# Attention with normalised q and k: per-stretch settings for the written-out order, one norm step fewer, pair scaling in the first group

## The chip, the cores and the metric

The kernel runs on 1 core of a Trainium2 chip. The core has five engines that run their own instruction streams and meet at semaphores: TensorE (PE in the profile; its weight loads are PEld), VectorE (DVE), ScalarE (ACT), GpSimd (POOL) and SyncE (SP), which here issues DMAs. The metric is the device time of one execution in microseconds (us); before the change it is 599.01 us, the median of 3 runs (598.86 to 599.35).

## The reference

32 heads, 2048 positions, 20 features a head, all bf16.

```python
qn = q / (jnp.sqrt((q * q).sum(axis=-1, keepdims=True)) + eps)
kn = k / (jnp.sqrt((k * k).sum(axis=-1, keepdims=True)) + eps)
logits = jnp.einsum('bhqd,bhkd->bhqk', qn, kn) * t[None, :, None, None]
attn = softmax(logits, axis=-1)
return jnp.einsum('bhqk,bhkd->bhqd', attn, v)
```

Since q and k have unit length and t is near 1, the logits are small, and the softmax needs no maximum: the kernel computes exp of the logits and divides at the end by their sum, which comes out of the same product as the result (v has a column of ones).

## The kernel before

**The work.** The heads go in 8 groups of 4 (hg), each group in 4 blocks of 512 queries: 32 blocks (sb). A block has 4 heads x 16 rows of 128 keys = 64 units. A unit is a score product (32 rows of TensorE, 128 keys by 512 queries, L802), the exp of its 128 x 512 scores, and the product of that with v (L824, accumulated in one PSUM bank per block). There are 32 x 64 = 2048 units, and each takes one of two ways:

- *A*: two units form a wave. Their scores go into half of psA, one ScalarE instruction (L1004) takes the exp of 128 x 1024 into pA, and each unit then has one product with v.
- *D*: the scores go into one of four banks of psD. VectorE turns them into int16 numbers dI (`P1`, L371) whose bits, read as f16, approximate an exp. GpSimd adds two constants to dI (`S1`, `S2`, L384), which gives two shifted copies dS. The weighted sum of the approximations is the exp, so this unit has four products with v: dI with vaug, dI with vhalf (half of v), and the two dS with vaug. The slots of dI and dS form a ring of 28.

When a block's products are done, VectorE drains the accumulator with a transpose (L396), takes reciprocals (L410), divides (L411), and SyncE's queue stores. For each group ahead of its use, q and k are loaded, squared (`sq`, L264), summed (by DMA transposes and small TensorE products with `ind`), and normed: an inverse square root from an integer guess `rs0` and a polynomial `rs1` to `rs5`, then `eps` and a reciprocal `inv` (L315 to L323). Then `rt` (L328) multiplies the norms by t and writes each twice, side by side, into rn2, so that the scaling `nmk` and `nmq` (L334) can read bf16 pairs; results go to kpad and qpad and from there through DMA transposes into kT and qT. The first group (hg 0) is done apart, in rows 0 to 4 (the norm by ScalarE's square root) and rows 4 to 16, k before q, with scalings of 4 rows an instruction straight from the f32 norms (L350). Rows 4 to 8 of k are transposed on TensorE (L667) and copied by VectorE (L673); the squares of the q part wait for that copy.

**What sets the order.** No engine decides anything on the chip. `make_plan` simulates the engines at build time on a clock of 0.005 us: each operation has a cost and a latency (an exp of a wave `ACT0 + 1024/1200` with ACT0 = .05, a dI `0.069 + 512/960`), each engine takes, when it is free, what its rules choose among what is ready, and the order of each engine's queue, DMAs included, is written out from that. Which units become waves and which go the D way comes out of the same simulation. (A second order without D units is written too, and runs only where the largest t is above a limit, which the kernel reads at its start; it doesn't run here.) Its rules have settings (`RULES`): `DURG`, `DFIRST` and `RUN` say when TensorE prefers D scores or products with v, `PVHOLD` how long before a free half of psA it stops starting products, `JOINB` when two neighbouring dI become one instruction of 1024, `PMIN` and `PGAP` when smaller rounds of products may run, `POOL_MAX` and `PSLACK` how many shifts GpSimd joins and how far they may outlast VectorE's dI, `BACK` when VectorE does shifts itself, `NEEDW` which head's units go to the waves, `PRIO` how urgent overdue norms are, and `TWICED` whether a D score is computed twice to keep TensorE busy. D units begin when 0.12 of the first group's units are issued (`D_FROM`).

Every ten waves the simulation reads one letter of `ORDER`, a number in base 36 that picks an entry of `CHOICES` to lay over the rules:

```python
if share and len(waves) // STRETCH > stretch:
    stretch = len(waves) // STRETCH
    vars(S).update(RULES, **CHOICES[int(ORDER[stretch:stretch + 1] or "0", 36)])
```

Before the change `ORDER` is empty: every stretch has entry 0, the plain rules. The lines the change touches are `RULES`/`CHOICES`/`ORDER` (top), `prep_ops` (norms and scalings), `ready_at`, `shift_ok` and the priorities of two small operations on tb2 in `t_load`.

Of the kernel before, what the change touches and what calls it, by code (L numbers as in the profile page):

```python
# [22 lines left out]
RS_C = (1.87956057, -1.25805744, 0.378493658)  # L23
# [4 lines left out]

RULES = dict(JOINB=2, JOINK=3, JOIN=0, DURG=1, RUN=1, PMIN=4, PGAP=0.4, PVHOLD=(.25, .25), DFIRST=1, PRIO=0.9, TWICE=1, TWICED=2, HEATD=0.8, HEATQ=0.75, HEAT=0.68, BACK=24, POOL_MAX=4, NEEDW=3, D_LAST=14, ALONE=(0,0), PSLACK=0.25, OLEND=8)
STRETCH = 10  # L30
CHOICES = ({}, dict(JOINB=1), dict(DURG=2), dict(RUN=2), dict(PVHOLD=(0, 0)), dict(PVHOLD=(.4, .4)), dict(DFIRST=0), dict(JOINB=1, JOIN=.15),
           dict(PRIO=1.1), dict(PMIN=3), dict(PGAP=.15), dict(JOINB=9), dict(TWICED=1), dict(TWICE=2, HEATQ=.6), dict(POOL_MAX=2), dict(DURG=0))
ORDER = ""

PARTS = ((0, 4), (4, 16))
NH = 4
# [43 lines left out]
POOL2 = .00166  # L80
SQ_ROWS = 1
SQN = 8
NM_ROWS = 4
SQ_POOL = False
POOL_S = 3
POOLPRIO = 3
# [70 lines left out]
def bass_standalone__qk_norm__prompt_kernel(  # L157
# [7 lines left out]
    B, H, S, D = q.shape  # L165
    assert B == 1 and D == 20 and S == 2048 and H % NH == 0, (B, H, S, D)
    R = S // 128
# [5 lines left out]
    with ExitStack() as es:  # L173
# [3 lines left out]
        tb16 = sbuf("tb16", [128, H], BF16)  # L177
# [52 lines left out]
        def ap(tile, base, *dims):  # L230
            return bass.AP(tile, base.offset, [base.ap[0]] + [list(d) for d in dims])


        def dve(name, n, rate, emit, reads, writes, ncols_fix=0.0, info=None):
            c = n * rate
            o = Op("DVE", name, emit, reads, writes, cost=0.069 + c + ncols_fix,
                   lat=0.135 + c + ncols_fix, info=info)

            o.port = name not in ("P1", "cp", "drain", "red", "inv", "rec")
            return o  # L240

        def pool_op(name, n, two, emit, reads, writes):
            c = POOL0 + n * (POOL2 if two else POOL1)
            return Op("POOL", name, emit, reads, writes, cost=c, lat=c + POOLL)
# [3 lines left out]
        def prep_ops(hg, r0, r1, a0=0, a1=2, pool=False):  # L248

            b = hg % 2  # L250
# [52 lines left out]
            def add(nm, emit, reads, writes, rate=R1, fix=0.0):  # L303
                ops.append(pool_op(nm, n, rate != R2, emit, reads, writes) if pool and nm in NORM_POOL else
                           dve(nm, n, rate, emit, reads, writes, fix))

            if nr == 4:
                n0 = nr0[:, :, :, :].rearrange("p a h r -> p (a h) r")
                ops.append(Op("ACT", "nrm", lambda e: e.activation(n0, s_, ACT.Sqrt), [SS], [K("ra")], 0.25, 0.3))
                add("eps", lambda e: e.tensor_scalar(ra, n0, 1e-6, None, ALU.add), [K("ra")], [K("ra")])  # L310
            else:

                y = ri.bitcast(F32)
                sums = lambda: psD[:, bank["at"] * QW:bank["at"] * QW + n].rearrange("p (h r) -> p h r", r=R) if hg else s_
                add("rs0", lambda e: e.tensor_scalar(ri, sums().bitcast(I32), -0.5, RS_MAGIC, ALU.mult, ALU.add), [SS], [K("ri")], R1 if hg else R2)  # L315
                add("rs1", lambda e: e.tensor_tensor(rb, sums(), y, ALU.mult), [K("ri"), SS], [K("rb")])
                bank["ops"] = ops[-2:]
                add("rs2", lambda e: e.tensor_tensor(ra, rb, y, ALU.mult), [K("ri"), K("rb")], [K("ra")])
                add("rs3", lambda e: e.tensor_scalar(s_, ra, RS_C[2], RS_C[1], ALU.mult, ALU.add), [K("ra")], [SS], R2)
                add("rs4", lambda e: e.tensor_tensor(s_, s_, ra, ALU.mult), [K("ra"), SS], [SS])  # L320
                add("rs5", lambda e: e.scalar_tensor_tensor(rb, s_, RS_C[0], rb, ALU.add, ALU.mult), [SS, K("rb")], [K("rb")])
                add("eps", lambda e: e.tensor_scalar(ra, rb, 1e-6, None, ALU.add), [K("rb")], [K("ra")], R2)
            add("inv", lambda e: e.reciprocal(rn_, ra), [K("ra")], RN[a0:a1], R1, n * 5 * R1)  # L323

            if hg:
                tt = ap(tb2, tb2[:, hg, :, :], [1, 2 * NH], [0, R], [0, 2])
                r_ = ap(rn[b], rn[b][:, :, :, :], [R, 2 * NH], [1, R], [0, 2])
                ops.append(dve("rt", 4 * NH * R, R1, lambda e: e.tensor_tensor(rn2[:, :, :, :, :].rearrange("p a h r x -> p (a h) r x"), r_, tt, ALU.mult),  # L328
                               [RN[0], RN[1], "tb2"], [("rn2", 0), ("rn2", 1)]))
                for a, pad, nm in ((1, kpad, "kpad"), (0, qpad, "qpad")):  # L330
                    src = ap(qk[b], qk[b][:, a, :, :, :], [R * D, NH], [D, R], [2, D // 2], [1, 2])
                    dst = ap(pad[b], pad[b][:, :, :, 0:D], [32, NH], [NH * 32, R], [2, D // 2], [1, 2])
                    sc = ap(rn2, rn2[:, a, :, :, :], [2 * R, NH], [2, R], [0, D // 2], [1, 2])
                    ops.append(dve("nm" + nm[0], NH * R * D, R2, lambda e, o=dst, x=src, s=sc: e.tensor_tensor(o, x, s, ALU.mult),  # L334
                                   [("qk", b, a, i) for i in parts] + [("rn2", a)] + [("qkx", b, i) for i in range(1, 4)] * (a == 0),
                                   [(nm, b, r) for r in range(R)]))
                return ops

            def scale(a, pad, nm, whole):
                step = NM_ROWS if r0 else 16  # L340
                for c0, c1 in [(c, min(c + step, r1)) for c in range(r0, r1, step)]:
                    nn = c1 - c0

                    base = qk[b][:, a, :, c0:c0 + nn, :]
                    src = bass.AP(qk[b], base.offset, [base.ap[0], [R * D, NH], [D, nn], [1, D]])
                    rb_ = rn[b][:, a, :, c0:c0 + nn]
                    sc = bass.AP(rn[b], rb_.offset, [rb_.ap[0], [R, NH], [1, nn], [0, D]])
                    db = pad[b][:, c0:c0 + nn, :, 0:D]
                    dst = bass.AP(pad[b], db.offset, [db.ap[0], [32, NH], [NH * 32, nn], [1, D]])
                    emit = lambda e, o=dst, x=src, s=sc: e.tensor_tensor(o, x, s, ALU.mult)  # L350
                    rd, wr = [("qk", b, a, i) for i in parts] + [RN[a]] + [("qkx", b, i) for i in range(1, 4)] * (a == 0), [(nm, b, r) for r in range(c0, c0 + nn)]
                    ops.append(pool_op("nm" + nm[0], 4 * nn * D, True, emit, rd, wr) if whole else
                               dve("nm" + nm[0], 4 * nn * D, R1, emit, rd, wr))

            if a1 == 2:
                scale(1, kpad, "kpad", False)
            if a0 == 0:
                rq = rn[b][:, 0, :, r0:r1]
                tt = bass.AP(tb16, tb16[:, hg * NH:(hg + 1) * NH].offset,
                             [tb16[:, :].ap[0], [1, NH], [0, nr]])  # L360
                emit = lambda e: e.tensor_tensor(rq, rq, tt, ALU.mult)
                ops.append(pool_op("rqt", 4 * nr, True, emit, [RN[0], "tb"], [RN[0]]) if pool else
                           dve("rqt", 4 * nr, R1, emit, [RN[0], "tb"], [RN[0]]))
                scale(0, qpad, "qpad", False)
            return ops

        def p1_op(pb, j, n):
# [111 lines left out]
        def make_plan(share):  # L479
# [2 lines left out]
            P = Plan()  # L482
            nsem[0] = n_sq[0] = 0
            SWITCH, SEML = 0.11, 0.06

            pA_ = lambda w, c, n: pA[:, c:c + n].bitcast(F16) if share and w else pA[:, c:c + n]
            units_of = lambda sb: {hh: [(sb, hh, r) for r in range(R)] for hh in range(NH)}
# [27 lines left out]
            pe_mode, grp, pe_t = None, [0.0] * 4, 0.0  # L515

            def ready_at(op):
                late = 0.4 if op.name == "drain" else 0.0
                return max([d.done + SEML + late for d in op.deps if d.done is not None] + [0.0]) \
                    if all(d.done is not None for d in op.deps) else None  # L520

# [62 lines left out]
            def t_load():  # L584
                src = bass.AP(t.tensor, 0, [[0, 128], [1, H]])
                want_sp(dma("ldt", lambda e: e.dma_start(tb16[:, :], src), [], ["tb"], 0.1, 3.2))  # L586
                want_dve(dve("flag", H, R1, lambda e: e.tensor_reduce(tmx[:, :], tb16[:, :], AXIS_X, ALU.max, apply_absolute_value=True), ["tb"], ["flag"]), 1.4)
                want_dve(Op("DVE", "z", lambda e: e.memset(tb2[:, :, :, :], 1.0), [], ["tb1"], 0.1, 0.2), 3)
                want_dve(dve("z", H, R1, lambda e: e.tensor_copy(tb2[:, :, 0, :], tb16[:, :].rearrange("p (g h) -> p g h", h=NH)), ["tb1", "tb"], ["tb2"]), 3)

            want_sp(load_qk(0, 1, 0)[0])
            o = P.link(load_qk(0, 0, 0)[0])
# [561 lines left out]
                return True  # L1154

            def shift_ok(x):
                return x[4].done is not None and x[4].done + SEML <= now and \
                    all(r.done is not None and r.done + SEML <= now for t_ in range(x[3]) for r in P.readers.get((f"dS{x[1]}", x[2] + t_), []))

            def shift_run():  # L1160
# [336 lines left out]
```

## Time and profile before

| | us |
|---|---|
| median of 3 runs | 599.01 (598.86 to 599.35) |
| the profiled execution, by the clock of the runs | 598.64 |
| its span, first to last instruction | 596.8 |
| busy: ScalarE, TensorE, VectorE, GpSimd | 583.9, 587.0, 574.3, 501.5 |

A profile line names the source line, engine and operation, what is written and read (out<-in), the count, busy time in us and the mean duration of one in ns, and the engine's idle time just before with what ended it. Busy time is the union of the durations; instructions on one engine overlap, so a mean can be longer than the distance from one to the next. TensorE's granted clock is 0.999 of full speed.

### The profile page before, as it was taken

How to read it: one execution, taken by the hardware profiler on the slowest of the kernel's cores; microseconds unless marked ns; L12 is line 12 of the kernel's file. 1: busy time of each engine (PE TensorE's matmuls, PEld its weight loads, DVE VectorE, ACT ScalarE, POOL GpSimd, SP SyncE). 2: the span in 40 equal slices, each digit the busy share in tenths (PEclk: the TensorE clock that was granted, in tenths of full speed). 3: DMA queues.
4: the chain of work that ended last, by engine and by line, in shares of the span. 5: the costliest groups of instructions: out<-in, count | busy, mean ns of one | idle time of the engine just before them, and what ended most of it. 6: DMA issues, size and time to landing. Idle time of an engine off the chain costs nothing.

```text
span 596.8 us, 16439 instructions
## 1 busy us (share of the span) xinstructions
PE 587.0 (98%) x6784; PEld 158.9 (27%) x6784; DVE 574.3 (96%) x1024; ACT 583.9 (98%) x640; POOL 501.5 (84%) x964
## 2 busy tenths in 40 slices
PE   8999999999999999999999999999999999999996
PEld 4432222322223222222222322222222222222221
DVE  7999999999999999999999999999999999999994
ACT  6999999999999999999999999999999999999994
POOL 2587998888988889888998879888898888999994
PEclk9999999999999999999999999999999999999999
DMA  8701405106060131502333042510505203010000
GB/s 117 106 2 34 83 2 68 24 1 116 4 88 3 28 88 14 78 3 43 74 25 67 1 47 72 69 23 1 99 3 62 45 8 66 3 23 7 7 2 16
DMA packets 132145, 24.20 MB, mean 41 GB/s; under 512 B 121312, under 2 KB 132064, under 8 KB 132064
## 3 DMA queue, kind: packets, MB, share of 16 engines
q1 hardware_dynamic: 131264, 22.96, 24.8%
q8 instruction: 55, 0.90, 0.6%
q14 instruction: 26, 0.21, 0.1%
q10 hardware_dynamic: 800, 0.12, 0.1%
HBM read 7.87 MB, written 2.62 MB: 18 GB/s over the span
## 4 chain that ended last, share of the span: by engine, by line
ACT 82%; PE 15%; SPq 1%; DMA 1%; DVE 0%; issue 0%
ACT pA L1004 82%; PE psD L824 8%; PE psA L802 6%; PE psD L802 1%; SPq L447 1%; DMA vaug<-in_v_dram 1%; SPq L437 0%; DVE accT L396 0%; PE psD L621 0%; DVE ost L411 0%; SPq L586 0%; DVE rec L410 0%
## 5 line engine op out<-in xcount | busy, mean ns | idle before, releaser
L1004 ACT ACTIVATE pA<-psA 128x1024 f16<-128x1024 f32 (+1 forms) x632 | 579.7, 1243 | 0.3 <-PE psA L802 0.2
L384 POOL INT64_ADD dS<-dI x948 | 495.2, 538 | 75.8 <-DVE dI L371 16.3
L371 DVE TENSOR_SCALAR dI<-psD 128x512 int16<-128x512 f32 (+1 forms) x765 | 485.9, 692 | 10.1 <-PE psD L802 7.3
L802 PE MATMUL psA<-qT,kT 32*128 32x512 bf16 x1264 | 247.9, 384 | 2.0 <-ACT pA L1004 0.6
L802 PE MATMUL psD<-qT,kT 32*128 32x512 bf16 x787 | 237.4, 383 | 0.3 <-DVE dI L371 0.2
L824 PE MATMUL psD<-dS,vaug 128*22 128x512 f16 x1568 | 201.8, 383 | 0.0
L824 PE MATMUL psD<-pA,vaug 128*22 128x512 f16 (+1 forms) x1264 | 183.2, 383 | 0.5 <-DMA vaug<-in_v_dram 0.5
L824 PE MATMUL psD<-dI,vaug 128*22 128x512 f16 x784 | 136.7, 383 | 0.0
L824 PE MATMUL psD<-dI,vhalf 128*22 128x512 f16 x784 | 133.6, 383 | 0.0
L802 PEld LDWEIGHTS psA<-qT,kT 32*128 32x128 bf16 x1264 | 59.4, 91 | 250.8 <-ACT pA L1004 245.7
L802 PEld LDWEIGHTS psD<-qT,kT 32*128 32x128 bf16 x787 | 56.7, 91 | 8.0 <-DVE dI L371 3.7
L824 PEld LDWEIGHTS psD<-dS,vaug 128*22 128x22 bf16 x1568 | 42.9, 89 | 56.8 <-issue 35.1
L824 PEld LDWEIGHTS psD<-pA,vaug 128*22 128x22 bf16 x1264 | 39.1, 89 | 48.3 <-issue 44.1
L824 PEld LDWEIGHTS psD<-dI,vaug 128*22 128x22 bf16 x784 | 30.0, 89 | 27.5 <-issue 22.4
L824 PEld LDWEIGHTS psD<-dI,vhalf 128*22 128x22 bf16 x784 | 29.0, 89 | 24.2 <-issue 16.3
L396 DVE STREAM_TRANSPOSE accT<-psD 128x512 f32<-128x512 f32 x32 | 22.5, 703 | 3.7 <-PE psD L824 3.7
L411 DVE TENSOR_TENSOR ost<-accT,rec 128x320 bf16<-128x320 f32 x32 | 17.0, 533 | 0.2
L621 PE MATMUL psD<-zt 128*128 128x128 bf16 x163 | 13.9, 221 | 0.0
L264 DVE TENSOR_TENSOR sqs<-qk 128x1280 bf16<-128x1280 bf16 x14 | 11.9, 851 | 0.0
L758 PE MATMUL psD<-ind,sqT 128*128 128x128 bf16 x140 | 11.5, 221 | 0.0
L621 PEld LDWEIGHTS psD<-zt 128*128 128x128 bf16 x163 | 9.4, 98 | 5.9 <-issue 5.9
L758 PEld LDWEIGHTS psD<-ind,sqT 128*128 128x128 bf16 x140 | 7.9, 98 | 5.0 <-issue 4.3
(61 smaller groups left out, 86.0 us busy)
## 6 DMA issues: line engine op xcount, KB each, us to landing
vaug<-in_v_dram SPq DMA_DIRECT2D x32, 80.0 KB, 4.2
qk<-in_k_dram SPq DMA_DIRECT2D x7, 320.0 KB, 4.1
out_dram<-ost SPq DMA_DIRECT2D x28, 80.0 KB, 1.9
qk<-in_q_dram SPq DMA_DIRECT2D x6, 320.0 KB, 4.2
qk<-in_q_dram SPq DMA_DIRECT2D x4, 80.0 KB, 3.5
out_dram<-ost SPq DMA_DIRECT2D x7, 40.0 KB, 2.1
qk<-in_k_dram SPq DMA_DIRECT2D x1, 240.0 KB, 3.7
qk<-in_q_dram SPq DMA_DIRECT2D x1, 240.0 KB, 4.3
```

What stands on the lines that cost most here:

```text
L264: ops.append(dve("sq", w_, R2, lambda e, o=sq, x=x3: e.tensor_tensor(o, x, x, ALU.mult), [("qk", b, a, i) for i in parts] + [("qkx", b, i) ...
L371: lambda e: e.tensor_scalar(dst, psD[:, pb * QW:(pb + n) * QW], 1024.0 * LOG2E, 15360.0 - 1024.0 * LOG2K + SHIFTS[0], ALU.mult, ALU.add),
L384: lambda e: e.int64_add(o.bitcast(U64), x.bitcast(U64), add), rd, wr)
L396: return dve("drain", QW, R1, lambda e: e.transpose(accT[:, 16 * b:16 * b + 16, :].rearrange("p b d -> p (b d)"), psO_(sb)), [("psD", OB(s ...
L411: dve("omul", 320 * n, R1, lambda e: e.tensor_tensor(dst, num, rcb, ALU.mult), at + ar, [("ost", hg % 2, g) for g in range(g0, g1)]),
L447: ops.append(dma("ldv", lambda e, d=d_, s=s_: e.dma_start(d, s), [], [("v", b, hh)], 1.4, 4.0))
L621: return lambda e: e.matmul(bank, zt[:, 0:128], zt[:, 0:n], start=False, stop=False, skip_group_check=True)
L758: mms = [lambda e, g=g, j=j: e.matmul(dst, sqT[:, (5 * g + j) * 128:(5 * g + j + 1) * 128], ind[:, j, 96 - 32 * g:224 - 32 * g], start=g + ...
L802: return lambda e: e.matmul(dst, lhsT, rhs, tile_position=(32 * hh, 0))
L824: return lambda e: e.matmul(dst, lhsT, rhs, start=first, stop=last, skip_group_check=True, tile_position=(0, 32 * hh))
L1004: a = Op("ACT", "exp", lambda e, s=src, d=dst: e.activation(d, s, ACT.Exp), [("psA", slot)], [("pA", pslot, i) for i in range(WAVES[slot]) ...
```

## The change

1. `CHOICES` has 23 entries instead of 16 (two old ones replaced), and `ORDER` is a string of 64 letters, one per ten waves.
2. In the simulation an operation counts as ready a little later than before: a dI by 0.015, an operation of GpSimd by 0.045 (`LATE`), and a shift is chosen 0.045 after its dI.
3. The polynomial of the norms is divided by its leading coefficient: `rs3` and `rs4` are now two instructions of the kind (a + c) x b, and `eps` multiplies by the coefficient while it adds 1e-6. One instruction fewer for each norm. The rows 0 to 4 of the first group, which use the square root, keep theirs.
4. Rows 4 to 16 of the first group get the pair form of the other groups: `rt` into rn2 (for k as well, with a factor 1) and one scaling of 12 rows each for k and q, in place of three of 4 rows; `rqt` goes there. tb2's two preparing operations get priority 1.45 instead of 3.

```diff
-CHOICES = ({}, ..., dict(JOINB=1, JOIN=.15), ..., dict(TWICE=2, HEATQ=.6), dict(POOL_MAX=2), dict(DURG=0))
-ORDER = ""
+CHOICES = ({}, dict(JOINB=1), dict(DURG=2), dict(RUN=2), dict(PVHOLD=(0, 0)), dict(PVHOLD=(.4, .4)), dict(DFIRST=0), dict(PVHOLD=(.33, .33)),
+           dict(PRIO=1.1), dict(PMIN=3), dict(PGAP=.15), dict(JOINB=9), dict(TWICED=1), dict(PVHOLD=(.15, .15)), dict(POOL_MAX=2), dict(DURG=0),
+           dict(PVHOLD=(.2, .3)), dict(PVHOLD=(.3, .2)), dict(NEEDW=1), dict(PSLACK=.1), dict(JOINB=1, DURG=2), dict(PVHOLD=(.2, .2), DURG=2), dict(BACK=12))
+ORDER = "0305080i2k7lj3700hj2e0me07cj08i7a1i0j01g2bjb5j5080i00g017fl67g60"
...
-                add("rs3", lambda e: e.tensor_scalar(s_, ra, RS_C[2], RS_C[1], ALU.mult, ALU.add), [K("ra")], [SS], R2)
-                add("rs4", lambda e: e.tensor_tensor(s_, s_, ra, ALU.mult), [K("ra"), SS], [SS])
-                add("rs5", lambda e: e.scalar_tensor_tensor(rb, s_, RS_C[0], rb, ALU.add, ALU.mult), [SS, K("rb")], [K("rb")])
-                add("eps", lambda e: e.tensor_scalar(ra, rb, 1e-6, None, ALU.add), [K("rb")], [K("ra")], R2)
+                add("rs3", lambda e: e.scalar_tensor_tensor(s_, ra, RS_C[1] / RS_C[2], ra, ALU.add, ALU.mult), [K("ra")], [SS])
+                add("rs4", lambda e: e.scalar_tensor_tensor(rb, s_, RS_C[0] / RS_C[2], rb, ALU.add, ALU.mult), [SS, K("rb")], [K("rb")])
+                add("eps", lambda e: e.tensor_scalar(ra, rb, RS_C[2], 1e-6, ALU.mult, ALU.add), [K("rb")], [K("ra")], R2)
...
+            def scale(a, pad, nm, c0, c1):
...
+                else:
+                    src = ap(qk[b], src, [R * D, NH], [D, nn], [2, D // 2], [1, 2])
+                    sc = ap(rn2, rn2[:, a, :, :, :], [2, NH * nn], [0, D // 2], [1, 2])
+                    dst = ap(pad[b], dst, [32, NH], [NH * 32, nn], [2, D // 2], [1, 2])
+                    rd, rate = rd + [("rn2", a)], R2
+                ops.append(dve("nm" + nm[0], 4 * nn * D, rate, lambda e: e.tensor_tensor(dst, src, sc, ALU.mult), rd, [(nm, b, r) for r in range(c0, c1)]))
...
+            t_ = ap(tb2, tb2[:, hg, a0:a1, :], [1, na * NH], [0, nr], [0, 2])
+            r_ = ap(rn[b], rn[b][:, a0:a1, :, r0:r1], [R, na * NH], [1, nr], [0, 2])
+            o_ = ap(rn2, rn2[:, a0:a1, :, :, :], [2 * nr, na * NH], [2, nr], [1, 2])
+            ops.append(dve("rt", 2 * n, R1, lambda e: e.tensor_tensor(o_, r_, t_, ALU.mult), RN[a0:a1] + ["tb2"], [("rn2", a) for a in range(a0, a1)]))
...
+            LATE = {"drain": 0.4, "P1": 0.015}
...
-                late = 0.4 if op.name == "drain" else 0.0
+                late = LATE.get(op.name, 0.045 if op.eng == "POOL" else 0.0)
...
-                return x[4].done is not None and x[4].done + SEML <= now and \
+                return x[4].done is not None and x[4].done + SEML + 0.045 <= now and \
```

More of the change, by code (lines that the diff above doesn't have):

```diff
@@ L30 @@
 STRETCH = 10
-CHOICES = ({}, dict(JOINB=1), dict(DURG=2), dict(RUN=2), dict(PVHOLD=(0, 0)), dict(PVHOLD=(.4, .4)), dict(DFIRST=0), dict(JOINB=1, JOIN=.15),
-           dict(PRIO=1.1), dict(PMIN=3), dict(PGAP=.15), dict(JOINB=9), dict(TWICED=1), dict(TWICE=2, HEATQ=.6), dict(POOL_MAX=2), dict(DURG=0))
-ORDER = ""
+CHOICES = ({}, dict(JOINB=1), dict(DURG=2), dict(RUN=2), dict(PVHOLD=(0, 0)), dict(PVHOLD=(.4, .4)), dict(DFIRST=0), dict(PVHOLD=(.33, .33)),
+           dict(PRIO=1.1), dict(PMIN=3), dict(PGAP=.15), dict(JOINB=9), dict(TWICED=1), dict(PVHOLD=(.15, .15)), dict(POOL_MAX=2), dict(DURG=0),
+           dict(PVHOLD=(.2, .3)), dict(PVHOLD=(.3, .2)), dict(NEEDW=1), dict(PSLACK=.1), dict(JOINB=1, DURG=2), dict(PVHOLD=(.2, .2), DURG=2), dict(BACK=12))
+ORDER = "0305080i2k7lj3700hj2e0me07cj08i7a1i0j01g2bjb5j5080i00g017fl67g60"
 PARTS = ((0, 4), (4, 16))
@@ L82 @@
 SQN = 8
-NM_ROWS = 4
 SQ_POOL = False
@@ L323, in prep_ops @@
+                add("rs4", lambda e: e.scalar_tensor_tensor(rb, s_, RS_C[0] / RS_C[2], rb, ALU.add, ALU.mult), [SS, K("rb")], [K("rb")])
+                add("eps", lambda e: e.tensor_scalar(ra, rb, RS_C[2], 1e-6, ALU.mult, ALU.add), [K("rb")], [K("ra")], R2)
             add("inv", lambda e: e.reciprocal(rn_, ra), [K("ra")], RN[a0:a1], R1, n * 5 * R1)
[L325 to L336, printed above, removed]
-                return ops
@@ L339, in scale @@
[L339 to L364, printed above, removed]
+            def scale(a, pad, nm, c0, c1):
+                nn = c1 - c0
+                src, dst = qk[b][:, a, :, c0:c1, :], pad[b][:, c0:c1, :, 0:D]
+                rd = [("qk", b, a, i) for i in parts] + [("qkx", b, i) for i in range(1, 4)] * (a == 0)
+                if nr == 4:
+                    src = ap(qk[b], src, [R * D, NH], [D, nn], [1, D])
+                    sc = ap(rn[b], rn[b][:, a, :, c0:c1], [R, NH], [1, nn], [0, D])
+                    dst = ap(pad[b], dst, [32, NH], [NH * 32, nn], [1, D])
+                    rd, rate = rd + [RN[a]], R1
+                else:
[4 more added lines that the diff above has]
+                ops.append(dve("nm" + nm[0], 4 * nn * D, rate, lambda e: e.tensor_tensor(dst, src, sc, ALU.mult), rd, [(nm, b, r) for r in range(c0, c1)]))
@@ new lines, in prep_ops @@
+            if nr == 4:
+                scale(1, kpad, "kpad", r0, r1)
+                rq = rn[b][:, 0, :, r0:r1]
+                t_ = ap(tb16, tb16[:, hg * NH:(hg + 1) * NH], [1, NH], [0, nr])
+                ops.append(dve("rqt", 4 * nr, R1, lambda e: e.tensor_tensor(rq, rq, t_, ALU.mult), [RN[0], "tb"], [RN[0]]))
+                scale(0, qpad, "qpad", r0, r1)
+                return ops
+            t_ = ap(tb2, tb2[:, hg, a0:a1, :], [1, na * NH], [0, nr], [0, 2])
+            r_ = ap(rn[b], rn[b][:, a0:a1, :, r0:r1], [R, na * NH], [1, nr], [0, 2])
@@ L365, in prep_ops @@
+            o_ = ap(rn2, rn2[:, a0:a1, :, :, :], [2 * nr, na * NH], [2, nr], [1, 2])
+            ops.append(dve("rt", 2 * n, R1, lambda e: e.tensor_tensor(o_, r_, t_, ALU.mult), RN[a0:a1] + ["tb2"], [("rn2", a) for a in range(a0, a1)]))
+            for a, pad, nm in ((1, kpad, "kpad"), (0, qpad, "qpad")):
+                if a0 <= a < a1:
+                    scale(a, pad, nm, r0, r1)
             return ops
@@ L587, in t_load @@
                 want_dve(dve("flag", H, R1, lambda e: e.tensor_reduce(tmx[:, :], tb16[:, :], AXIS_X, ALU.max, apply_absolute_value=True), ["tb"], ["flag"]), 1.4)
-                want_dve(Op("DVE", "z", lambda e: e.memset(tb2[:, :, :, :], 1.0), [], ["tb1"], 0.1, 0.2), 3)
-                want_dve(dve("z", H, R1, lambda e: e.tensor_copy(tb2[:, :, 0, :], tb16[:, :].rearrange("p (g h) -> p g h", h=NH)), ["tb1", "tb"], ["tb2"]), 3)
+                want_dve(Op("DVE", "z", lambda e: e.memset(tb2[:, :, :, :], 1.0), [], ["tb1"], 0.1, 0.2), 1.45)
+                want_dve(dve("z", H, R1, lambda e: e.tensor_copy(tb2[:, :, 0, :], tb16[:, :].rearrange("p (g h) -> p g h", h=NH)), ["tb1", "tb"], ["tb2"]), 1.45)
             want_sp(load_qk(0, 1, 0)[0])
```

## The prediction

> **What bounds the kernel now.** I read the page first (busy shares, chain, groups), then one tile's instructions, the waits, the windows.
>
> ```profile
> span 596.8 us, 16439 instructions
> PE 587.0 (98%) x6784; PEld 158.9 (27%) x6784; DVE 574.3 (96%) x1024; ACT 583.9 (98%) x640; POOL 501.5 (84%) x964
> ACT 82%; PE 15%; SPq 1%; DMA 1%; DVE 0%; issue 0%
> L1004 ACT ACTIVATE pA<-psA 128x1024 f16<-128x1024 f32 (+1 forms) x632 | 579.7, 1243 | 0.3 <-PE psA L802 0.2
> L384 POOL INT64_ADD dS<-dI x948 | 495.2, 538 | 75.8 <-DVE dI L371 16.3
> L371 DVE TENSOR_SCALAR dI<-psD 128x512 int16<-128x512 f32 (+1 forms) x765 | 485.9, 692 | 10.1 <-PE psD L802 7.3
> L824 PE MATMUL psD<-dI,vaug 128*22 128x512 f16 x784 | 136.7, 383 | 0.0
> ```
>
> ScalarE's exps are the floor. Four engines look nearly full, but only this one has no holes: 632 waves of two units take 579.7 together, 0.917 each, with 0.3 of idle time ahead of them. (A mean of 1243 ns beside that pitch says that each starts before the last has ended.) The other 784 units, the count of products of dI with vaug, go through VectorE; 2 x 632 + 784 = 2048 is all the work. So the time is a head, 0.917 for every wave, and a tail. Their bounds:
>
> ```profile
> L1004 ACT ACTIVATE pA<-psA x632: 1017/1246/1346, 8.8 to 587.4; 128x1024 f16<-128x1024 f32 x157, 128x1024 bf16<-128x1024 f32 x1
> 586.42 2.15 ACT L1004 ACTIVATE pA<-psA 128x1024 f16<-128x1024 f32 x2
> 586.27 0.54 PE psD L824 x8
> 587.39 3.59 PE psD L824 x63
> ```
>
> The first exp starts at 8.8, the last ends at 586.42 + 2.15 = 588.57, and what follows until 596.8 takes 8.2; TensorE works off products until 587.39 + 3.59 = 590.98 of it. This execution took 598.64 by the clock of the runs, 0.37 below their median of 599.01; I work out differences against it and put them on the median.
>
> The time can fall by fewer waves, which means more units for VectorE and GpSimd, or by a shorter head or tail. What room those two engines have is read where the dI line runs:
>
> ```profile
> 22.86:587.31 564.45, 562.79 (x6540) 147.09 (x6536) 554.15 (x955) 564.45 (x617) 493.50 (x945) 1.00 0.24 38
> 25.00:50.00 25.00, 24.83 (x290) 6.96 (x291) 24.39 (x46) 25.00 (x28) 22.65 (x45) 1.00 0.11 22
> 50.00:75.00 25.00, 24.55 (x289) 7.09 (x285) 23.67 (x39) 25.00 (x29) 20.80 (x43) 1.00 0.39 69
> ...
> 175.00:200.00 25.00, 25.00 (x296) 7.09 (x292) 23.81 (x45) 25.00 (x29) 20.55 (x38) 1.00 0.09 18
> ...
> 250.00:275.00 25.00, 24.95 (x301) 7.01 (x293) 25.00 (x49) 25.00 (x29) 21.66 (x42) 1.00 0.12 25
> ...
> 375.00:400.00 25.00, 24.95 (x288) 7.63 (x284) 23.74 (x39) 25.00 (x28) 21.50 (x44) 1.00 0.42 54
> ...
> 550.00:575.00 25.00, 24.96 (x287) 6.11 (x283) 24.58 (x42) 25.00 (x29) 23.67 (x46) 1.00 0.03 5
> DVE dI L371 <- PE psD L802: 7.3, 22, 0.8
> POOL dS L384 <- DVE dI L371: 16.3, 45, 6.5
> 564.67 10.44 DVE L371 TENSOR_SCALAR dI<-psD 128x512 int16<-128x512 f32 x17
> ```
>
> The columns behind the length of a window are PE, PEld, DVE, ACT, POOL. VectorE is idle for 564.45 - 554.15 = 10.3, nearly all ahead of dI and 7.3 of it in 22 waits for a score matmul. It isn't evenly spread: three windows of 25 us lose 1.2 to 1.3 each, the best none. GpSimd waits for dI for 16.3, 6.5 of them once, so it lacks work for about 9.8.
>
> **Part 1, the order.** The 64 letters change no instruction. They change which unit goes which way and what stands ahead of what on every engine and on the DMA queues, since one simulated clock places all of them. What one wave fewer is worth: an exp, 0.917, goes. Two units more go to VectorE, at (10.44 - 0.68) / 16 = 0.61 each by the run of 17 (the last one's own 0.68, its usual length, taken off); that is 1.22 more work in 0.917 less time, so it uses up 2.14 of VectorE's idle time. Four shifts more go to GpSimd, 493.50 / 1568 = 0.315 each (two for each of 784 units): 1.26 + 0.917 = 2.18 of its idle time. TensorE gets six products more, 6/8 of 0.54 = 0.41, and loses one turn of scores for an exp, of about the same length; I cost it at nothing. Its cover is that the exps hardly wait for it now; where that is gone, each late turn is at most the 0.8 of the longest wait above.
>
> How much idle time will a better order close? At worst none, or it opens more; at best all 10.3. Settings that change every ten waves, that is every 9.2 us, can mend the bad stretches. The typical window of the 22 between 25 and 575 loses about 0.37; the ones above it, the three named foremost (1.33, 1.26 and 1.19), lose 4.0 in excess of that. I take 4.0, because those windows differ from the best ones in order alone.
>
> **Part 2, norms in one instruction fewer.** For 7 groups, four instructions on 128 x 128 become three:
>
> ```profile
> L319 DVE TENSOR_SCALAR ssum<-rsa 128x128 f32<-128x128 f32 x7 | 1.7, 246 | 0.0
> L320 DVE TENSOR_TENSOR ssum<-ssum,rsa 128x128 f32<-128x128 f32 x7 | 2.1, 302 | 0.0
> L321 DVE SCALAR_TENSOR_TENSOR rsb<-ssum,rsb 128x128 f32<-128x128 f32 x7 | 2.1, 307 | 0.0
> L322 DVE TENSOR_SCALAR rsa<-rsb 128x128 f32<-128x128 f32 x7 | 1.7, 240 | 0.0
> ```
>
> Two of the kind of L321 and one of L322 take the place of all four: L319's 1.7 goes, and L320 turns into a twin of L321 for nothing. Instructions of VectorE overlap by some 0.07 to 0.09 (dI: 0.68 long, 0.61 apart), so the real gain is nearer 1.7 - 7 x 0.08 = 1.1. At least nothing, at most 1.7; I take 1.1, all of it idle time won for part 1.
>
> **Part 3, the first group scaled in pairs.**
>
> ```profile
> 4.93 0.17 DVE L589 CAST tb<-tb 128x32 f32<-128x32 bf16 x1
> 4.95 0.23 ACT L309 ACTIVATE nr<-ssum 128x32 f32<-128x32 f32 x1 [2.11 <-DVE ssum L294]
> ...
> 11.03 0.19 DVE L319 TENSOR_SCALAR ssum<-rsa 128x48 f32<-128x48 f32 x1
> 11.25 0.21 DVE L320 TENSOR_TENSOR ssum<-ssum,rsa 128x48 f32<-128x48 f32 x1
> 12.45 1.30 DVE L350 TENSOR_TENSOR kpad<-qk,rn 128x320 bf16<-128x320 bf16 x3
> 14.27 0.69 DVE L673 CAST kT<-psD 128x512 bf16<-128x512 f32 x1 [0.53 <-PE psD L667]
> 19.49 0.21 DVE L361 TENSOR_TENSOR rn<-rn,tb 128x48 f32<-128x48 f32 x1
> 19.74 1.30 DVE L350 TENSOR_TENSOR qpad<-qk,rn 128x320 bf16<-128x320 bf16 x3
> 22.22 0.39 PE L802 MATMUL psD<-qT,kT 32*128 32x512 bf16 x2
> 22.86 1.88 DVE L371 TENSOR_SCALAR dI<-psD 128x512 int16<-128x512 f32 x3
> L334 DVE TENSOR_TENSOR kpad<-qk,rn 128x1280 bf16<-128x1280 bf16 x7 | 5.8, 830 | 0.0
> ```
>
> For q: one norm step fewer (0.22, from 11.03 to 11.25), rt in place of rqt (about even), and three scalings of 1.30 together become one of 960 elements in pairs, 830 x 960/1280 = 0.62: 0.9 sooner. But the first score for dI stands at 22.22 + 0.39 = 22.61, and that is set by the share of units issued, not by VectorE; so dI can start at 22.6 instead of 22.86, and 0.25 is won. For k nothing: the scaling ends about 0.2 later for its first rows (rt added, one long instruction where a short one came first) and 0.4 earlier for the last, but the copy of kT waits 0.53 for TensorE's transposes anyway, and the q part waits for that copy. Should those transposes slip by the 0.2, kT is there at 15.2; its first use is the ninth wave, at 8.8 + 8 x 0.917 = 16.1. The DMA transposes of kT's and qT's later rows are released 0.4 and 0.9 sooner, which nothing waits for: the exps have no hole there. The head up to the first exp keeps its instructions; the copy into tb2 (L589), which gets an earlier turn, already runs beside the square root on ScalarE, and out of that cover it would cost the head its 0.17. Part 3 is worth 0 to 0.9 of VectorE's time; I take 0.25.
>
> **Part 4, the corrected lengths.** They add no instruction and act through the order alone: a dI and a shift count as ready 0.015 and 0.045 later. They lie in part 1's bounds.
>
> **The sum.** 4.0 + 1.1 + 0.25 = 5.35 of idle time, at 2.14 a wave, is 2.5 waves: 2 or 3 fewer, -2.3. For the tail I take one pair of product rounds less after the last exp, -0.5, between +1 and -1.9 (all that TensorE does from 588.57 to 590.98 but one such pair). -2.8 in all: 595.8 by this execution, 596.2 on the median.
>
> The Trainium skill, page "ScalarE: Activation LUTs", section "What ACT_TABLE_LOAD costs", gives 186 ns + 0.833 ns an element for an ACTIVATE with immediates and an overlap of 93 ns, an estimate of 0.946 a wave. The trace's 0.917 differs and decides; by the page the waves would be worth -2.4.
>
> **Rivals.**
> 1. *Slower: the order saves what the chip doesn't lack.* The simulation gives an exp 0.05 + 1024/1200 = 0.903, the trace 0.917; so it sees gaps between exps that the chip fills. An order that closes those puts waves ahead of dI and shifts units to ScalarE. Each wave more is +0.917; from two more it decides: +1.8, 600.8. For it: exps wait only 0.3 here, so nothing is to be had from them. Against: VectorE's holes above are in the same simulated order and would show there too.
> 2. *No change: GpSimd becomes the bound.* Its 9.8 lasts for 9.8 / 2.18 = 4.5 waves, if it can be reached; with the order of before its waits beside VectorE's short SBUF instructions (75.8 - 16.3 = 59.5) can't be used. If those grow, shifts come late, the ring of dI slots stays full, and the waves stay 632 plus or minus one: 599.0. The Trainium skill, page "SBUF — State Buffer", section "SBUF: two separate sides", says that GpSimd is shut out for the whole of a VectorE instruction with two SBUF inputs; the waits counted here agree in kind, and no row shows how long one lock lasts.
> 3. *Much faster: nearly all of the idle time closes.* (10.3 + 1.1 + 0.25) / 2.14 = 5.4 waves by VectorE, 4.5 by GpSimd: 5 fewer, -4.6, with 1 off the tail 593.4.
>
> **How the numbers follow.** Forecast 0.44, rival 3 0.18, rival 2 0.19, rival 1 0.19. Within 0.2% (1.2 us) a measurement here can't tell a change. So faster 0.62, same 0.19, slower 0.19. The forecast's own range is 594.5 to 597.5 (2 to 3 waves, tail from +0.3 to -1.7). The range for 8 in 10 reaches down to 592.5, rival 3 with all 1.9 of the tail, and up to 600.2, two thirds of the way to rival 1.
>
> **What would show it.** Count the exps: 629 or 630, at a pitch of still 0.917; dI products 788 or 790. Idle time ahead of dI near 6 instead of 10.1. Four lines of norms become three of L321's and L322's length. First exp at 8.8, first dI near 22.6. Products after the last exp end under 2.4 behind it. I am wrong if the exps number 632 or more, or if idle time ahead of them grows past 1: then TensorE, late with scores, sets the pace, and a saved wave pays for a stall.

## The result and the profile after

The changed kernel takes 596.25 us, the median of 6 runs (595.59 to 596.56), beside 598.95 of the kernel before: a ratio of 0.9953, with a 95% interval of 0.994 to 0.9966. The profiled execution took 596.55 by the clock of the runs, with a span of 594.4; the one before lay 0.37 below its median and this one 0.30 above, so the pair of profiles shows 2.4 of span where the medians show 2.7. Two slow runs of the kernel before, beside no_order, norms_pairs, shuffled and warm, took 797.68 and 606.64 (granted clock 0.558 and 0.983), and since the second counts in the ratios of these four, their ratios are about 0.0013 lower than those of the medians (599.08 before).

The page after, those lines of it that answer to the ones shown of before (busy time of each engine, chain, groups):

```profile
span 594.4 us, 16322 instructions
PE 582.6 (98%) x6741; PEld 154.0 (26%) x6741; DVE 574.4 (97%) x1012; ACT 582.3 (98%) x638; POOL 498.2 (84%) x947
ACT 83%; PE 13%; SPq 1%; POOL 1%; DMA 1%; DVE 1%; issue 0%
L995 ACT ACTIVATE pA<-psA 128x1024 f16<-128x1024 f32 (+1 forms) x630 | 578.1, 1254 | 1.8 <-PE psD L793 0.9
L374 POOL INT64_ADD dS<-dI x931 | 491.8, 544 | 77.6 <-DVE dI L361 14.6
L361 DVE TENSOR_SCALAR dI<-psD 128x512 int16<-128x512 f32 (+1 forms) x764 | 488.1, 695 | 8.1 <-PE psD L793 5.6
L815 PE MATMUL psD<-dI,vaug 128*22 128x512 f16 x788 | 130.6, 382 | 0.0
```

There are 630 exps instead of 632, still 578.1 / 630 = 0.918 each, and 788 units went through VectorE instead of 784. But the exps now stand still for 1.8 (0.3 before). VectorE's uneven windows did close: the three named in the prediction are idle for 0.41, 0.11 and 0.25 instead of 1.33, 1.19 and 1.26, but the one from 25 to 50 for 1.81 instead of 0.61. Where the exps begin and end, and what comes after them, in three views: the instructions on tile pA, ScalarE's timeline, and the chain at the end.

```profile
L995 ACT ACTIVATE pA<-psA x630: 1018/1262/1346, 8.6 to 587.1; 128x1024 f16<-128x1024 f32 x157, 128x1024 bf16<-128x1024 f32 x1
```

```profile
28.66 5.98 ACT L995 ACTIVATE pA<-psA 128x1024 f16<-128x1024 f32 x6 [0.92 <-PE psD L793]
584.26 4.05 ACT L995 ACTIVATE pA<-psA 128x1024 f16<-128x1024 f32 x4
```

```profile
587.09 1.69 PE psD L815 x28
588.80 0.73 DVE accT L386
```

The last exp ends at 584.26 + 4.05 = 588.31, where it ended before (588.57), although two waves are gone: the holes took them back. What was won lies behind it. TensorE ends its products at 588.78, 0.5 after the last exp instead of 2.4, and from the last exp to the end of the span it is 6.1 instead of 8.2. So the span's 2.4 are made of: head -0.2 (8.6 instead of 8.8), waves -1.8, holes +1.8, tail -2.2 (6.07 instead of 8.24).

The longest hole ends at 28.66: 1.0 is lost there, and 0.4 more until 33.5. TensorE's queue there, and GpSimd's instructions of the shift line (two answers of the trace, of the changed kernel):

```profile
26.08 0.39 PE L793 MATMUL psD<-qT,kT 32*128 32x512 bf16 x2
27.91 0.39 PE L815 MATMUL psD<-dS,vaug 128*22 128x512 f16 x4 [1.43 <-POOL dS L374]
28.23 0.39 PE L793 MATMUL psA<-qT,kT 32*128 32x512 bf16 x2
```

```profile
L374 POOL INT64_ADD dS<-dI x931: 387/398/1065, 25.6 to 587.0; - x187
L374 POOLq MODIFY_POOL_CONFIG  x2: 11/11/11, 19.0 to 19.0; - x2
```

The scores of the next wave (28.23) stand behind products with dS (27.91), and those wait 1.43 for GpSimd. GpSimd's first shift starts at 25.59. The dI that it needs starts at 22.90, takes 0.69, and so has been there since 23.59: the wait that the profile puts down to dI is something else. The rows point to one thing: at 19.0, 0.8 after the group's zeros are written, GpSimd's sequencer changes its configuration, and the first shift comes 6.6 later. The kernel before has the same, at 18.8 and 24.44, 5.7 apart, but there TensorE's queue reached the products with dS at 26.99 and did not wait for them:

```profile
L384 POOL INT64_ADD dS<-dI x948: 387/398/1042, 24.4 to 588.1; - x190
L384 POOLq MODIFY_POOL_CONFIG  x2: 11/11/11, 18.7 to 18.8; - x2
```

```profile
26.99 0.75 PE L824 MATMUL psD<-dS,vaug 128*22 128x512 f16 x8
```

A second hole has nothing to do with GpSimd. Four waves after the first exp, the scores stand behind the first product with v, and that waits for its load (both rows of the changed kernel):

```profile
11.87 0.40 PE L815 MATMUL psD<-pA,vaug 128*22 128x512 bf16 x4 [0.91 <-DMA vaug<-in_v_dram]
```

```profile
12.90 8.43 ACT L995 ACTIVATE pA<-psA 128x1024 f16<-128x1024 f32 x9 [0.56 <-PE psA L793]
```

So a shorter head only waits longer there: 8.57 + 0.56 here and 8.97 + 0.16 in the kernel called warm below come to the same 9.13. The kernel before had no such hole behind its 8.80. The head's -0.2 is thus no gain, and about 0.4 of the 1.8 that the holes grew by belongs to v.

### The profile page after: what moved, and what is told of

Same layout as the page of the kernel before. It is cut to its first block, busy times and chain, and to the rows that moved or that the text cites. A ratio compares the mean times of both kernels' runs of the same rounds, so it can differ in the third digit from the quotient of the medians.

```text
span 594.4 us, 16322 instructions
## 1 busy us (share of the span) xinstructions
PE 582.6 (98%) x6741; PEld 154.0 (26%) x6741; DVE 574.4 (97%) x1012; ACT 582.3 (98%) x638; POOL 498.2 (84%) x947
## 4 chain that ended last, share of the span: by engine, by line
ACT 83%; PE 13%; SPq 1%; POOL 1%; DMA 1%; DVE 1%; issue 0%
ACT pA L995 83%; PE psD L815 7%; PE psA L793 5%; POOL dS L374 1%; PE psD L612 1%; SPq L437 1%; DMA vaug<-in_v_dram 1%; PE psD L793 1%; DVE dI L361 0%; SPq L427 0%; DVE accT L386 0%; DVE ost L401 0%; SPq L577 0%; PE psD L658 0%; DVE rec L400 0%
## 5 line engine op out<-in xcount | busy, mean ns | idle before, releaser
L995 ACT ACTIVATE pA<-psA 128x1024 f16<-128x1024 f32 (+1 forms) x630 | 578.1, 1254 | 1.8 <-PE psD L793 0.9
L793 PE MATMUL psA<-qT,kT 32*128 32x512 bf16 x1260 | 245.2, 384 | 2.2 <-ACT pA L995 0.8
L793 PE MATMUL psD<-qT,kT 32*128 32x512 bf16 x793 | 240.7, 383 | 0.1
L815 PE MATMUL psD<-dS,vaug 128*22 128x512 f16 x1576 | 196.3, 383 | 1.4 <-POOL dS L374 1.4
L815 PE MATMUL psD<-pA,vaug 128*22 128x512 f16 (+1 forms) x1260 | 172.5, 383 | 1.1 <-DMA vaug<-in_v_dram 0.9
L815 PE MATMUL psD<-dI,vaug 128*22 128x512 f16 x788 | 130.6, 382 | 0.0
L815 PE MATMUL psD<-dI,vhalf 128*22 128x512 f16 x788 | 128.6, 383 | 0.0
L815 PEld LDWEIGHTS psD<-pA,vaug 128*22 128x22 bf16 x1260 | 36.7, 89 | 49.3 <-issue 45.4
L386 DVE STREAM_TRANSPOSE accT<-psD 128x512 f32<-128x512 f32 x32 | 22.6, 705 | 2.7 <-PE psD L815 2.7
L612 PE MATMUL psD<-zt 128*128 128x128 bf16 x106 | 9.2, 221 | 0.0
L322 DVE RECIPROCAL rn<-rsa 128x128 f32<-128x128 f32 (+2 forms) x10 | 7.8, 780 | 0.1
```

Source lines behind the costliest of these rows:

```text
L386: return dve("drain", QW, R1, lambda e: e.transpose(accT[:, 16 * b:16 * b + 16, :].rearrange("p b d -> p (b d)"), psO_(sb)), [("psD", OB(s ...
L612: return lambda e: e.matmul(bank, zt[:, 0:128], zt[:, 0:n], start=False, stop=False, skip_group_check=True)
L793: return lambda e: e.matmul(dst, lhsT, rhs, tile_position=(32 * hh, 0))
L815: return lambda e: e.matmul(dst, lhsT, rhs, start=first, stop=last, skip_group_check=True, tile_position=(0, 32 * hh))
L995: a = Op("ACT", "exp", lambda e, s=src, d=dst: e.activation(d, s, ACT.Exp), [("psA", slot)], [("pA", pslot, i) for i in range(WAVES[slot]) ...
```

## The experiments

My theory 1 was that the letters make the gain, through waves and tail, and that the hole is GpSimd's late start, not TensorE. Against it stood that the saved instructions make the gain (theory 2), that the letters carry over to other simulations (theory 3), and that the letters themselves make the hole (theory B below). Ratios are to the kernel before, on the same chip.

**Norms and pairs without letters, with and without the corrected lengths.**

```diff
-ORDER = "0305080i2k7lj3700hj2e0me07cj08i7a1i0j01g2bjb5j5080i00g017fl67g60"
+ORDER = ""
```

For norms_pairs also:

```diff
-            LATE = {"drain": 0.4, "P1": 0.015}
+            LATE = {"drain": 0.4}
-                late = LATE.get(op.name, 0.045 if op.eng == "POOL" else 0.0)
+                late = LATE.get(op.name, 0.0)
-                return x[4].done is not None and x[4].done + SEML + 0.045 <= now and \
+                return x[4].done is not None and x[4].done + SEML <= now and \
```

> The changed kernel with an empty ORDER: norms, pairs and corrected lengths alone. The order written out has 632 waves, as many as before. Theory 1 (the letters make the gain, by waves and by the tail): no gain, 598.3 to 599.5. Theory 2 (VectorE's saved instructions make the gain, the letters hardly matter): about 596.3, as with the letters.

> The kernel before with norms and pairs alone: empty ORDER and the lengths of before. 632 waves. Theory 1: 598.3 to 599.3; VectorE's norm lines take some 1.4 us less in total and nothing else moves, since two units are needed to save a wave. Theory 2: 596.3. The difference to no_order is what the corrected lengths do without letters: under 0.7 by theory 1.

no_order: 599.84, ratio 1.0 (0.9972 to 1.0028). norms_pairs: 599.05, ratio 0.9988 (0.9959 to 1.0017). norms_pairs is no faster than the kernel before (599.08 there). no_order missed its range by 0.3: all its ten runs lie between 599.49 and 600.51, 0.8 above the kernel before by the medians, and 0.8 above norms_pairs where under 0.7 was expected. Neither gains, so theory 2 falls: the saved instructions alone make no time, and the letters are worth 3.6 (599.84 against 596.25). In no_order the exps also wait 0.59 and 0.36 behind products with GpSimd's first shifts, so that hole needs no letters; the longer of the two waits comes first here, then the group of the exps in norms_pairs, and VectorE's norms:

```profile
29.24 1.94 ACT L995 ACTIVATE pA<-psA 128x1024 f16<-128x1024 f32 x2 [0.59 <-PE psD L793]
```

```profile
L995 ACT ACTIVATE pA<-psA 128x1024 f16<-128x1024 f32 (+1 forms) x632 | 579.8, 1209 | 0.9 <-PE psA L793 0.6
```

```profile
L319 DVE SCALAR_TENSOR_TENSOR ssum<-rsa 128x128 f32<-128x128 f32 x7 | 2.0, 290 | 0.0
L320 DVE SCALAR_TENSOR_TENSOR rsb<-ssum,rsb 128x128 f32<-128x128 f32 x7 | 2.1, 304 | 0.0
L321 DVE TENSOR_SCALAR rsa<-rsb 128x128 f32<-128x128 f32 x7 | 1.7, 240 | 0.0
L338 DVE TENSOR_TENSOR kpad<-qk,rn 128x960 bf16<-128x960 bf16 x1 | 0.7, 658 | 0.0
```

The four lines of 7.6 became three of 5.8, as the change says, and a scaling in pairs takes 0.66 where three took 1.30. But 632 waves stay 632 waves.

**The same letters elsewhere.** In shuffled they stand in another, random order; in letters_before they are given, with the new CHOICES, to the kernel before, with none of the rest.

```diff
-ORDER = "0305080i2k7lj3700hj2e0me07cj08i7a1i0j01g2bjb5j5080i00g017fl67g60"
+ORDER = "j0770a7660i00fcjle05b580l071i873ggkmj2jjjeb00i0100228i00h5g30107"
```

> The changed kernel with its 64 letters in another, random order. 634 waves come out. Theory 1 (the letters were picked for their places, and any other set of them is a random one): two waves more than before, 600.5 to 602. Rival (varied settings are better than one setting throughout): 597 or less.

> The kernel before with the new CHOICES and the 64 letters, but without norms, pairs and corrected lengths. 634 waves come out, two more than with empty letters. Theory 1 (the letters are a sequence that fits one simulation only; every change of a length makes them random): 600 to 601.5. Theory 3 (the letters find the bad places of the work itself and carry over): 597.5 or less.

shuffled: 601.76, ratio 1.0031 (1.0002 to 1.006), 634 waves: as theory 1 has it, though the two waves are only 1.8 of the 2.7 by the medians. In its profile the product with the first v waits 1.8 for its load, and the exps wait 1.4 there; theory 1 had no term for that. letters_before: 599.13, ratio 1.0006 (0.9997 to 1.0016), also 634 waves. There my number was missed by 0.9: the two waves more cost what they should, but the tail came out short. The chain's products behind the last wave, and the last exps on the timeline, in letters_before:

```profile
589.67 2.08 PE psD L825 x36
```

```profile
584.13 6.71 ACT L1005 ACTIVATE pA<-psA 128x1024 f16<-128x1024 f32 x7
```

The last exp ends at 590.84, 2.3 later than before (1.8 of it the two waves, most of the rest a hole behind v), and the products 0.9 after it instead of 2.4. Waves and tail are thus two things that letters set, and neither follows from the other. Theory 3 falls for the time and the waves: no gain is carried over. The short tail is there in both kernels with these letters; whether it carried over or came by chance, one case doesn't tell.

**An early 64-bit addition on GpSimd.** A tile of 4 columns is added to once, ahead of everything but the first memsets; the order is otherwise the same.

```diff
+        wu = sbuf("wu", [128, 4], I16)
...
+            w = P.link(Op("POOL", "wu", lambda e: e.int64_add(wu[:, :].bitcast(U64), zt[:, 0:4].bitcast(U64), 0), ["zt"], ["wu"], 0.4, 0.5))
+            finish(w, free_["POOL"], w.cost, w.lat)
+            free_["POOL"] += w.cost
```

> The changed kernel with one small 64-bit addition (4 columns of a zeroed tile into a tile of its own) on GpSimd right after its first memsets; the order is otherwise the same, 630 waves. In the changed kernel GpSimd's first shift starts at 25.59, 2.0 after the end of the dI it waits for (23.59), and the exps stand still for 1.0 at 28.7 and 0.4 more until 33.6. Theory A (the first 64-bit addition of a program starts late on GpSimd, whatever it waits for): with the early one the first shift starts within 0.6 of its dI, the exps keep their pitch, 594.7 to 595.2. Theory B (the letters ask for the products with dS too early): the hole at 28.7 stays, 596.0 to 596.5.

> The kernel before with the early 64-bit addition on GpSimd, the order otherwise the same, 632 waves. Before, GpSimd's first shift starts 0.9 after its dI and the exps have no hole there. If the early addition helps only by taking away holes between exps: no change, 598.6 to 599.3. If it sped up the shifts in general: 597.9 or less, as much as it gave the changed kernel.

warm: 595.28, ratio 0.9924 (0.9896 to 0.9953). A second time, beside the kernels below: 594.87, 0.9926 (0.9909 to 0.9942). warm_before: 598.61, ratio 0.9994 (0.9985 to 1.0004). The groups of warm, its shift line, and the line of the early addition:

```profile
L999 ACT ACTIVATE pA<-psA 128x1024 f16<-128x1024 f32 (+1 forms) x630 | 577.8, 1257 | 0.4 <-PE psA L797 0.4
L362 DVE TENSOR_SCALAR dI<-psD 128x512 int16<-128x512 f32 (+1 forms) x764 | 488.0, 695 | 6.7 <-PE psD L797 4.3
```

```profile
L375 POOL INT64_ADD dS<-dI x931: 395/401/1057, 23.7 to 585.6; - x187
```

```profile
L552 POOLq MODIFY_POOL_CONFIG  x2: 12/12/12, 4.3 to 4.3; - x2
L552 POOL INT64_ADD wu<-zt x1: 190/190/190, 4.4 to 4.4; - x1
```

Theory A holds. The configuration is changed once, at 4.3, and no more at 19; the first shift starts at 23.70, 0.1 after its dI (22.91 + 0.69), the hole at 28.7 is gone, and the exps wait 0.4 in all. The time gained is 1.0, and 1.4 the second time, where I had expected 1.1 to 1.6; 595.28 is just outside the range of theory A, 594.87 inside. In warm_before the first shift came just as promptly (23.7) and no time was won, since no exp waited for it.

**A simulation corrected by the traces, with letters of its own.** The trace of the exps gives three rules: ends are 0.9165 apart where nothing is waited for (nearly all lie between 0.915 and 0.918), a start may lie 0.43 ahead of the last end (the durations run from 1017 to 1346), and scores follow an end. The simulation instead starts an exp when the last one's 0.903 are over and counts each late one as lost. clock_a, clock_b and clock_empty get these rules, a later landing of the first v, and the early addition; a and b have letters picked anew for them, empty has none.

```diff
+                if a.name == "exp":
+                    end = max(exp_end[0] + .9165, now + 1.025)
+                    a.cost, a.lat = max(.904, end - .43 - now), end - now
+                    exp_end[0] = end
...
-                ops.append(dma("ldv", ..., [("v", b, hh)], 1.4, 4.0))
+                ops.append(dma("ldv", ..., [("v", b, hh)], 1.4, 4.0 if hg else 5.5))
```

> The kernel with the early 64-bit addition, its simulation corrected by the traces: exps end 0.9165 apart at the least and may start 0.43 before the last one has ended; the first group's v counts as landed 1.5 later, so that no product stands ahead of it in TensorE's queue. New letters, picked one after the other by the simulated time and work left. 630 waves. Theory (time is head, 0.917 a wave, holes and tail): no hole at 13.9, tail about 6.2: 8.6 + 630 x 0.917 + 6.2 = 592.5 of span, 594.2. Rival (the hole behind v moves to another place, or other holes open where letters are new): 595 to 596.

> As clock_a with other letters, found from another start; 630 waves. Theory: 594.2, within 0.5 of clock_a, since letters matter only through waves, holes and tail. Rival: letters of equal waves differ by more than 1.

> As clock_a with empty letters: 634 waves. Theory: 8.6 + 634 x 0.917 + 8.3 (the long tail of empty letters) = 598.3 of span, 600.0. Rival (a truer exp in the simulation is itself worth the waves): 597 or less.

> The kernel of warm once more, beside the three others on one chip: 595.0 to 595.6, so that clock_a and clock_b can be compared with it.

clock_a: 595.2, ratio 0.993 (0.9913 to 0.9947). clock_b: 594.78, 0.9922 (0.9905 to 0.9938). warm_again: 594.87. clock_empty: 600.72, 1.0025 (1.0015 to 1.0035). The tile of the exps in clock_a, then the group of clock_empty:

```profile
L1000 ACT ACTIVATE pA<-psA x630: 1017/1218/1345, 9.7 to 586.0; 128x1024 f16<-128x1024 f32 x157, 128x1024 bf16<-128x1024 f32 x1
```

```profile
L1000 ACT ACTIVATE pA<-psA 128x1024 f16<-128x1024 f32 (+1 forms) x634 | 581.3, 1209 | 0.2 <-PE psA L798 0.2
```

In clock_a the 629 pitches from the first start to the last are (586.0 - 9.7) / 629 = 0.916: nothing is left between the exps, yet the kernel can't be told from warm, and it missed its 594.2. That time lies in the range of the rival, but no hole is there. Its first exp starts at 9.7 where the others' start between 8.4 and 9.5. The first loads of k and q land within 0.15 of each other in all these executions, and VectorE has the scaled q between 6.9 and 7.2; but TensorE's transposes stand behind 17 products of zeros, and those last between 0.38 and 0.63 each. In no_order, with the earliest first exp, most are short, in clock_a most are long (least, median and longest in ns):

```profile
L616 PE MATMUL psA<-zt x17: 379/379/634, 1.6 to 6.3; 128*128 128x512 bf16 x17
L621 PE MATMUL psA<-zt x17: 379/634/634, 1.7 to 7.9; 128*128 128x512 bf16 x17
```

These instructions are the same in both kernels; what makes them short or long, no run here shows. The four runs of clock_a took 594.45, 594.56, 595.84 and 596.13, and the profile is of 595.84. clock_b missed 594.2 as well, by 0.6, and is within 0.5 of clock_a, as expected of equal waves. clock_empty took 0.7 more than expected, again with a late first exp (9.2). It shows that a truer exp in the simulation is by itself worth nothing: without letters it made 634 waves. All kernels with 630 waves and no long hole lie between 594.8 and 595.3.

All profiled executions in one view (us; the exps' stretch is from the first start to the last end, holes are what is left of it after 0.917 a wave; the -0.1 show how exact that is):

| kernel | first exp | waves | stretch | holes | after the last exp | span |
|---|---|---|---|---|---|---|
| before | 8.80 | 632 | 579.8 | 0.2 | 8.2 | 596.8 |
| after | 8.57 | 630 | 579.7 | 2.0 | 6.1 | 594.4 |
| norms_pairs | 9.50 | 632 | 580.5 | 0.9 | 7.8 | 597.8 |
| no_order | 8.35 | 632 | 581.6 | 2.0 | 8.8 | 598.7 |
| shuffled | 8.53 | 634 | 583.7 | 2.4 | 8.2 | 600.4 |
| letters_before | 8.69 | 634 | 582.2 | 0.8 | 6.4 | 597.2 |
| warm_before | 8.51 | 632 | 580.3 | 0.7 | 8.0 | 596.8 |
| warm | 8.97 | 630 | 578.0 | 0.2 | 6.5 | 593.4 |
| warm_again | 8.89 | 630 | 578.2 | 0.4 | 5.9 | 593.0 |
| clock_a | 9.69 | 630 | 577.6 | -0.1 | 6.7 | 594.0 |
| clock_b | 8.63 | 630 | 578.0 | 0.3 | 7.1 | 593.7 |
| clock_empty | 9.23 | 634 | 581.3 | -0.1 | 8.3 | 598.8 |

## Why the prediction was right or wrong

The number, the direction and the range were right: 596.2 forecast, 596.25 measured. Three of the terms under it were not: by the two profiles the waves were worth 0.5 less than forecast, the holes cost 1.8 that the sum put at nothing, and the tail gave 1.7 more. That these cancelled is luck. Of the prediction's own signs, 630 exps, 788 products, the pitch and the short tail came. The idle time ahead of dI came to 8.1 instead of near 6, and the first dI at 22.90 instead of 22.6. One sign of being wrong came too: the exps' idle time grew past 1, to 1.8, though not for want of TensorE's time.

- *Head, 0.917 a wave, tail.* Held in every kernel of the table; the pitch is 0.918 after the change too. The 0.946 that I worked out from the Trainium skill's "ScalarE: Activation LUTs", section "What ACT_TABLE_LOAD costs", is not what this trace shows.
- *2.5 waves fewer.* There were 2, -1.8 instead of -2.3. The step behind it, idle time divided by 2.14 a wave, can be tested where no hole disturbs it: two waves use up 4.3, and the idle time before plus the norms' gain (10.3 + 1.3) less 4.3 leaves 7.3; warm is idle for 562.79 - 555.86 = 6.9 from its first dI on. So the price fits, and the sum's 5.35 was too much: two waves used 4.3 of it. The 4.0 that I took out of the uneven windows was a guess of the right size, no more.
- *Norms, 1.1 of VectorE's time.* The four lines' 7.6 became 2.1 + 2.1 + 1.5 = 5.7 in the changed kernel; less the overlap of one instruction, 7 x 0.08, that is 1.3. Right; and no time by itself, as no_order and norms_pairs show. Whether the letters could have saved two waves without it wasn't tried.
- *Pairs, 0.25.* The scaling was sized right (0.66 for 0.62), the gain was not there: dI starts at 22.90, not at 22.6, after 0.88 of waiting for its score, which TensorE placed at 22.43 instead of 22.22. The step that failed is that this score's place stays: it goes by the units issued, as the prediction had it, and the waves' scores ahead of it were late by the same 0.2 (21.39 instead of 21.17). VectorE's time in the head went to waste entirely.
- *No holes.* This is the step that failed most: "I cost it at nothing", with 0.8 as the most that a late turn could take. The exps lost 1.8 instead, some 0.4 of it behind the first v. The turn that was late was not a score for lack of TensorE's time but a product behind GpSimd's first shift; it waited 1.43, and the exps lost about 1.4 by it. The bound of 0.8 was VectorE's longest wait, for a score, and says nothing of a product that waits for GpSimd. The early addition shows it: without the second change of configuration the long hole is gone and the holes are back at 0.2 (0.4 the second time), and 1.0 to 1.4 of time with them. The rows for this lay in the trace of before (18.8 and 24.44 on the shift line); I had set GpSimd's 6.5 of waiting there aside as a single wait for dI, without asking why the shift came 0.9 after it.
- *Tail, -0.5.* It was -2.2; 1.9 of that in products left over after the last exp, all that the bound allowed. The rest lies behind the products, where two executions of one kernel differ by as much as 0.6 (warm 6.5 and 5.9 after the last exp). I mis-sized it because I took one pair of rounds as typical; with the letters 28 products were left in the last batch instead of 63, and without them, in no_order, the tail is 8.8 again.
- *Rival 1* (the simulation's short exp misleads the order) did not come about: the waves went down, not up, and with a true exp and no letters there were 634. *Rival 2*, GpSimd as the bound, came about once, not for want of speed but for one late start. *Rival 3* wanted five waves fewer; no letters tried saved more than two, and without the hole that is worth 594.8 to 595.3.

The version that beats both kernels is warm: four lines more, 595.28 and 594.87, which by the medians is 0.9937 and 0.9930 of the time before.

## What to carry to other kernels

Where one engine runs without holes, write the time as its head, its count times its pitch, its holes and its tail, and ask of each change which of the four it moves; savings on another engine are worth nothing until they change the count. Settings found for a written-out order belong to the lengths that they were found with: given to the kernel with other lengths, they gained nothing here. And look at the first use of a kind of instruction on GpSimd (here the 64-bit addition): put a small one early, where nothing waits for it.

## What the runs showed of the hardware that I had not expected

After a change of its configuration GpSimd's next instruction can come as late as some 6 us. Between `MODIFY_POOL_CONFIG` and the first 64-bit addition lie 5.7 (before) and 6.6 (after), though what the addition waits for came 0.9 and 2.0 earlier; in the four other kernels without the early addition it is 5.7 to 6.4. The mask selection of the head changes the configuration too, at 4.2, and then runs at 11.4 (6.4 in warm), which the profile puts down to a norm step of VectorE:

```profile
L540 POOLq MODIFY_POOL_CONFIG  x2: 11/11/11, 4.2 to 4.3; - x2
L540 POOL TENSOR_SCALAR_AFFINE_SELECT ind<-ind x2: 342/345/348, 11.4 to 11.8; 128x160 bf16<-128x160 bf16 x2
```

The Trainium skill, page "GPSIMD Engine Reference", section "2.1 Instruction dispatch", says that `ModifyPoolConfig` can load new code and that the first call to freshly loaded code pays about 6 us with no instruction to show for it. The two distances agree with that. With the 64-bit addition first, the change is made once, at 4.3, the addition follows at 4.4 without any such wait, and the selection comes at 6.4 with no change of its own. That the code was still there from the execution before would explain it; no run here shows that.
